# Nyström attention and a gated MLP: Newton inverses of batches 3+4 and 5+6 taken together, query weights kept unsplit until late, squares summed sooner

## The chip, the cores and the metric

One core of one Trainium2 chip. The metric is the device time of one execution in microseconds. "L563" and the like below are line numbers of the kernel file; PE is TensorE, DVE VectorE, ACT ScalarE, POOL GpSimd, SP SyncE (here it only issues DMAs).

## The reference

```python
# q, k, v: 8 batches x 8 heads x 576 tokens x 64; m = 32 landmarks of 18 tokens
q_lm, k_lm = means of q and k over the 18 tokens of each landmark
A, Bm, C = sm(q, k_lm), sm(q_lm, k_lm), sm(q_lm, k)          # softmax of scale*a@b.T
Z = Bm.T / (norm1(Bm) * norminf(Bm) + 1e-6)
for _ in range(6):
    Z = 2 * Z - Z @ Bm @ Z
x = (A @ Z @ C @ v)                                          # -> 4608 tokens x 512
xn = x / sqrt(mean(x * x) + 1e-6) * rms_g
out = (silu(xn @ w_gate) * (xn @ w_val)) @ w_out             # 512 -> 1536 -> 512
```

All of it is float32. The kernel gets this precision on PE by writing a number as a sum of two fp32r parts (hi and lo) and taking three products: hi by hi, hi by lo, lo by hi.

## The kernel before, in words

**Two parts.** The first part, which the change touches, runs the attention of all 8 batches and, mixed into it, the MLP of the first 4 of 12 blocks of 128 hidden units, for all tokens. The tokens come in 9 chunks of 512 (chunk i needs the attention of batches up to i, each of 576 tokens); eight chunks, 0 to 7, are run in this part by `mlp_chunk`. A chunk is 144 matmuls of 128x512: four blocks with 12 for the gate (psg) and 12 for the value (psv), then 48 for the output (pso). Its first matmul reads xhi, the hi part of the normalized tokens of kk = 0, its second xlo. The second part (the remaining blocks, from about 505 us on) is not touched.

**The attention of a batch** is a chain of steps; a batch's 8 heads form two groups g of 4 heads.

- `stage1(b, g)`: landmarks lmT (L342, sums on DVE of q and k, 128x1152 each), the next group's loads of q, k and v, then the scores sC and sA (16 small matmuls and 4 for psB), maxima mx (L376), E = exp(sC) on ACT, Bm (L392), and tA, sA transposed by DVE (L395).
- `back(b, g)`: softmax of tA: mA (L406), subtraction on POOL (L407), exp on ACT, sums, product on POOL (L414), transposition to AT (L416), and its split into AS, hi by ACT (L418) and lo by DVE (L419); transposes of E on PE (sE, sF), and pCV = C v, scaled into PV (L443).
- `newton(b)`: once both groups are through stage1, the start of Z, p0 on PE; once both groups are through back, five steps of 8 small matmuls (pn, 32x96) and one DVE operation (L498), which carry Z and Z C v together; a sixth for the product alone; then pW, split into Whi and Wlo.
- `second(b)`: pO (24 matmuls, AS by Whi and Wlo), copied by ACT into xr (L554), squared on ACT into sq; pss, the sum of squares over channels (8 matmuls); sqT, its transposition (L563); pms, which adds up four partial rows (L569); then on DVE ms, r, a reciprocal square root by ten small operations (L571 to L581), Rb, Rt (L583, L585), and xr scaled in place, four operations (L587). xr is stored to DRAM (xd, L591), and `finish` casts it to xhi on ACT (L614) and subtracts for xlo on DVE and POOL (L616).

**What sets the order.** Each engine runs its instructions in the order in which the program gives them. The steps above are generators, called streams; a `Mixer` keeps a clock, adds 0.216 for each MLP matmul (`MMT`), and after each lets one stream go on whose time has come. What a stream yields is how much work it added and how long it then waits; these waits are constants such as `OWL` (7.0: the wait between the last pO of a batch and its pss, times a slack of 1.3). Streams also wait for stages: stage1 of batch b for the Newton steps of batch b - 2, second(b) for newton(b) and for chunk b - 1 to have begun. After chunk i's last matmul the mixer is drained until second(i + 1) is through. The streams of second and newton run at high priority.

**Memory.** PE's results of the attention go through 5 banks of PSUM (tag pa), those of the MLP through 3 (tag pg). xr, E, tA, q/k and v have two buffers each, AT one, AS four.

Of the kernel before, what the change touches and what calls it, by code (L numbers as in the profile page):

```python
# [35 lines left out]
OWL = 7.0  # L36
# [13 lines left out]
TAB = 2  # L50
# [25 lines left out]
TINY = 1.0513759e-09  # L76


@with_exitstack
def nystrom_moe_kernel(  # L80
# [47 lines left out]
    VZ = cst.tile([P, G, 3 * D], F32, name="VZ")  # L128
# [169 lines left out]
    with tc.tile_pool(name="ap", bufs=1, side="right") as ap, tc.tile_pool(  # L298
# [36 lines left out]
        def stage1(b, g):  # L335
            nt = state[b]
            qk = loaded.pop((b, g))
            vt, vl_ = loaded.pop((b, g, "v"))
# [7 lines left out]
            if b > 0 and nxt[0] < B:  # L346
                load_qk(*nxt)
                load_v(*nxt)
# [31 lines left out]
            E = ap.tile([P, S], F32, name="E", tag="E", bufs=2)  # L380
# [4 lines left out]
            eb = sm.tile([P, M], F32, name="eb", tag="eb")  # L385
# [6 lines left out]
            (nc.scalar.mul if BMA else nc.vector.tensor_scalar_mul)(nt["Bm"][:, g, :], eb, rs[:, 1:2])  # L392
            tA = ap.tile([P, NB, M], F32, name="tA", tag="tA", bufs=TAB)
            for e in range(2):
                nc.vector.transpose(  # L395
                    tA[:, e * (NB // 2) : (e + 1) * (NB // 2), :].rearrange("p n m -> p (n m)"),
                    sA[e],
                )
            yield 1.3, 0.0
            if g == 1:  # L400
                stage["front"] = b

            def back():
                yield -BW * mix.slack
                mA = sm.tile([P, NB], F32, name="mA", tag="mA")
                nc.vector.tensor_reduce(mA, tA, axis=AX.X, op=ALU.max)  # L406
                nc.gpsimd.tensor_sub(tA, tA, mA.unsqueeze(2).broadcast_to([P, NB, M]))  # L407
                nc.scalar.activation(tA, tA, AF.Exp, scale=SC)
                sumA = sm.tile([P, NB], F32, name="sumA", tag="sumA")
                nc.vector.tensor_reduce(sumA, tA, axis=AX.X, op=ALU.add)  # L410
                nc.vector.tensor_scalar_add(sumA, sumA, 1e-9)
                rA = sm.tile([P, NB], F32, name="rA", tag="rA")
                nc.vector.reciprocal(rA, sumA)
                nc.gpsimd.tensor_mul(tA, tA, rA.unsqueeze(2).broadcast_to([P, NB, M]))  # L414
                AT = ap.tile([P, S], F32, name="AT", tag="AT", bufs=ATB)
                nc.vector.transpose(AT, tA.rearrange("p n m -> p (n m)"))  # L416
                AS = ap.tile([P, 2, S], F32R, name="AS", tag="AS", bufs=ASB)
                nc.scalar.copy(AS[:, 0], AT)  # L418
                nc.vector.tensor_sub(AS[:, 1], AT, AS[:, 0].bitcast(F32))  # L419
                nt["AT"][g] = AS  # L420

                sE = pa.tile([P, 4, P], F32, name="sE", tag="pa")
                for ch in range(4):
                    tp(sE[:, ch], E[:, ch * P : (ch + 1) * P], ident)
                sF = pa.tile([2 * M, P], F32, name="sF", tag="pa")
                tp(sF, E[:, 4 * P :], ident)
                ET = ap.tile([P, 4, P], F32, name="ET", tag="ET", bufs=ETB)
                EL = ap.tile([2 * M, P], F32, name="EL", tag="EL", bufs=ETB)
                nc.scalar.copy(ET, sE)
                nc.scalar.copy(EL, sF)  # L430
                yield 0.65, SW2
                pCV = pa.tile([P, D], F32, name="pCV", tag="pa")
                for ch in range(5):
                    for h in range(4):
                        r = slice(h * M, (h + 1) * M)
                        mm(
                            pCV[r, :],
                            ET[:, ch, r] if ch < 4 else EL[:, r],
                            vt[:, h, ch, :] if ch < 4 else vl_[:, h, :],
                            start=(ch == 0),  # L440
                            stop=(ch == 4),
                        )
                (nc.scalar.mul if CVA else nc.vector.tensor_scalar_mul)(nt["PV"][:, g, M:], pCV, rs[:, 0:1])  # L443
                yield 0.85, 0.2
                done[b] = done.get(b, 0) + 1
                if done[b] == 2:
                    stage["first"] = b

            mix.add(back())
# [9 lines left out]
        def newton(b):  # L459
            nt = state[b]  # L460
            Bm = nt["Bm"]
            BT = sm.tile([P, 2, M], F32, name="BT", tag="BT", bufs=1)
# [28 lines left out]
            yield 0.35, 0.0
            while stage["first"] < b:
                yield -0.3
            yield 0.0, NS
            for _ in range(5):
                pn = bmm(PV[:, :, :M], PV, M + D, "pn")
                PVn = sm.tile([P, 2, M + D], F32, name="PV", tag="PV", bufs=3)
                nc.vector.scalar_tensor_tensor(PVn, PV, 2.0, pn, op0=ALU.mult, op1=ALU.subtract)  # L498
# [3 lines left out]
            nc.vector.scalar_tensor_tensor(  # L502
                VZ[:, :, D : 2 * D], PV[:, :, M:], 2.0, pn, op0=ALU.mult, op1=ALU.subtract
            )
            yield 0.45, NP
            Whi = sm.tile([P, 2, P], F32R, name="Whi", tag="Whi", bufs=1)
            Wlo = sm.tile([P, 2, P], F32R, name="Wlo", tag="Wlo", bufs=1)
            pW = pa.tile([P, 2, P], F32, name="pW", tag="pa")
            for g in range(2):
# [12 lines left out]
            nt["W"] = Whi, Wlo  # L522
            yield 0.5, WW

        def new_state(b):
            state[b] = {
                "Bm": sm.tile([P, 2, M], F32, name="Bm", tag="Bm"),
                "PV": sm.tile([P, 2, M + D], F32, name="PV", tag="PV", bufs=3),
                "AT": [None, None],
            }  # L530

        def first(b):
            new_state(b)
            for g in range(2):
                yield from stage1(b, g)
# [3 lines left out]
        def second(b):  # L539
            nt = state.pop(b)  # L540
            (Whi, Wlo), ATs = nt["W"], nt["AT"]
            xr = ap.tile([P, NK, S], F32, name="xr", tag="xr", bufs=2)
            sq = ap.tile([P, NK, S], F32, name="sq", tag="sq", bufs=1)
            for g in range(2):
                po = [[pa.tile([P, HS], F32, name="pO", tag="pa") for j in range(2)] for e in range(2)]
                for e in range(2):
                    for n, (w, a) in enumerate(((Whi, 0), (Whi, 1), (Wlo, 0))):
                        for j in range(2):
                            r = slice(j * D, (j + 1) * D)
                            cols = slice(e * HS, (e + 1) * HS)  # L550
                            mm(po[e][j], w[r, g], ATs[g][r, a, cols], start=(n == 0), stop=(n == 2))
# [125 lines left out]
        mix.add(newtons(), True)  # L677
        mix.add(early.stream(WAIT0, NCV))
# [375 lines left out]
```

## Time and profile before

| what | value |
|---|---|
| time, median of 3 runs | 1066.85 us (1066.61 to 1067.96) |
| profiled execution | 1064.71 us, span 1062.8 us |
| chunks 0 to 3 begin at | 67.10, 134.10, 200.60, 268.80 us |
| chunk 7, without attention | 443.60 to 476.20 us |
| mean granted clock of PE | 0.961 |

A row of the timeline is start, duration, engine, line, operation, result and sources, shapes, count, and in brackets the idle time of the engine ahead of it and what ended that. A row of the windows has for each engine its busy time, then the granted clock of PE (1.00 is full), the share of DMA and GB/s. The waits list what PE waited for: total, number, the longest. A matmul's printed duration overlaps with the next, so the distance between two starts is its cost.

### The profile page before, as it was taken

How to read it: one execution, taken by the hardware profiler on the slowest of the kernel's cores; microseconds unless marked ns; L12 is line 12 of the kernel's file. 1: busy time of each engine (PE TensorE's matmuls, PEld its weight loads, DVE VectorE, ACT ScalarE, POOL GpSimd, SP SyncE). 2: the span in 40 equal slices, each digit the busy share in tenths (PEclk: the TensorE clock that was granted, in tenths of full speed). 3: DMA queues.
4: the chain of work that ended last, by engine and by line, in shares of the span. 5: the costliest groups of instructions: out<-in, count | busy, mean ns of one | idle time of the engine just before them, and what ended most of it. 6: DMA issues, size and time to landing. Idle time of an engine off the chain costs nothing.

```text
span 1062.8 us, 17582 instructions
## 1 busy us (share of the span) xinstructions
PE 992.8 (93%) x6918; PEld 833.9 (78%) x6918; DVE 743.4 (70%) x1503; ACT 486.7 (46%) x990; POOL 89.5 (8%) x86
## 2 busy tenths in 40 slices
PE   5639689989989999999999999999999999999998
PEld 3326466556767777787989899998999989899997
DVE  7799586797494551988995675747897475675743
ACT  3534556555454543455645352433744334352431
POOL 2243121211020210100000000000000000000000
PEclk7659889999999999999999999999999999999999
DMA  9244343434140211543533505134250432505122
GB/s 335 100 150 136 133 164 105 153 104 163 43 142 11 86 45 40 187 145 119 189 123 135 178 1 179 51 129 155 64 178 21 159 96 83 179 1 178 50 70 80
DMA packets 62946, 123.82 MB, mean 117 GB/s; under 512 B 5520, under 2 KB 27024, under 8 KB 61840
## 3 DMA queue, kind: packets, MB, share of 16 engines
q1 hardware_dynamic: 62864, 122.71, 34.0%
q8 instruction: 54, 0.88, 0.3%
q14 instruction: 28, 0.23, 0.1%
HBM read 84.94 MB, written 37.75 MB: 115 GB/s over the span
## 4 chain that ended last, share of the span: by engine, by line
PE 72%; DVE 15%; DMA 6%; issue 2%; ACT 2%; POOL 2%; SPq 0%; ACTq 0%; POOLq 0%; DVEq 0%
PE pso L141 23%; PE px L141 18%; PE pz L141 9%; PE psg L141 6%; PE psv L141 5%; PE pw L141 5%; DMA qk<-in_q_dram 2%; PE pO L141 2%; DMA srawv<-in_moe_w_val_dram 1%; DVE lmT L342 1%; PE pn L141 1%; DVE xr L587 1%; DVE h L275 1%; PE sC L141 1%; PE pss L141 1%
## 5 line engine op out<-in xcount | busy, mean ns | idle before, releaser
L141 PE MATMUL pso<-whio,h 128*128 128x512 f32 x288 | 96.2, 402 | 5.8 <-DVE h L275 4.7
L141 PE MATMUL pso<-solo,h 128*128 128x512 f32 x432 | 100.4, 390 | 0.0
L829 ACT CAST x<-xf 128x768 fp32r<-128x768 f32 x84 | 68.1, 833 | 69.7 <-DVE xf L847 54.2
L141 PEld LDWEIGHTS pso<-solo,h 128*128 128x128 f32 x432 | 81.0, 188 | 16.3
L141 PE MATMUL pso<-sowhio,h 128*128 128x512 f32 x288 | 90.9, 390 | 0.0
L141 PE MATMUL psg<-xhi,whig 128*128 128x512 f32 x144 | 60.7, 421 | 25.6 <-ACT xhi L614 25.6
L945 DVE TENSOR_TENSOR ob<-ob,pso 128x512 f32<-128x512 f32 x72 | 48.8, 684 | 49.1 <-PE pso L141 48.1
L830 DVE TENSOR_TENSOR x<-xf,x 128x768 fp32r<-128x768 f32 x84 | 79.2, 953 | 5.0 <-ACT x L829 5.0
L877 DVE TENSOR_TENSOR h<-c,h 128x384 fp32r<-128x384 f32 x96 | 53.2, 555 | 37.3 <-ACT h L876 37.2
L898 ACT COPY c<-px 128x384 f32<-128x384 f32 x48 | 23.1, 481 | 108.6 <-PE px L141 108.6
L141 PEld LDWEIGHTS pso<-whio,h 128*128 128x128 f32 x288 | 53.4, 188 | 20.4 <-DVE h L275 6.0
L876 ACT CAST h<-c 128x384 fp32r<-128x384 f32 x96 | 49.4, 515 | 34.5 <-DVE c L887 28.3
L141 PE MATMUL psg<-xlo,whig 128*128 128x512 f32 x144 | 60.6, 421 | 4.7 <-DVE xlo L616 4.0
L141 PEld LDWEIGHTS pso<-sowhio,h 128*128 128x128 f32 x288 | 54.1, 188 | 11.0
L141 PE MATMUL psg<-xhi,wlog 128*128 128x512 f32 x144 | 60.5, 420 | 0.0
L141 PE MATMUL psv<-xhi,wlov 128*128 128x512 f32 x144 | 58.1, 403 | 0.0
L141 PE MATMUL px<-x,swfs0c 128*128 128x384 f32 x288 | 58.0, 335 | 0.0
L141 PE MATMUL psv<-xlo,whiv 128*128 128x512 f32 x144 | 58.0, 403 | 0.0
L141 PE MATMUL px<-x,swfs1c 128*128 128x384 f32 x288 | 57.8, 334 | 0.1
L141 PE MATMUL px<-x,swfs2c 128*128 128x384 f32 x288 | 57.8, 335 | 0.0
L141 PE MATMUL psv<-xhi,whiv 128*128 128x512 f32 x144 | 57.8, 401 | 0.0
L141 PE MATMUL pso<-wloo,h 128*128 128x512 f32 x144 | 57.4, 398 | 0.0
(224 smaller groups left out, 2231.6 us busy)
## 6 DMA issues: line engine op xcount, KB each, us to landing
xd<-xr SPq DMA_DIRECT2D x8, 1152.0 KB, 4.3
pd<-ob SPq DMA_DIRECT2D x36, 256.0 KB, 2.1
xf<-xd SPq DMA_DIRECT2D x8, 1152.0 KB, 7.5
ob<-pd SPq DMA_DIRECT2D x36, 256.0 KB, 3.5
pe<-ob SPq DMA_DIRECT2D x36, 256.0 KB, 2.6
ob<-pe SPq DMA_DIRECT2D x36, 256.0 KB, 2.8
out_dram<-ob SPq DMA_DIRECT2D x36, 256.0 KB, 2.7
vt<-in_v_dram SPq DMA_DIRECT2D x16, 512.0 KB, 4.0
```

The source lines that it names most:

```text
L141: tc.keep_in_program_order(nc.tensor.matmul(*args, **kw))
L275: nc.vector.tensor_sub(h2, s, h1.bitcast(F32))
L342: nc.vector.tensor_reduce(lmT[:, z], qk[z].rearrange("p h (m c) -> p h m c", c=LM), axis=AX.X, op=ALU.add)
L587: last = nc.vector.scalar_tensor_tensor(xr[:, kk], xr[:, kk], gsb[:, kk : kk + 1], Rt, op0=ALU.mult, op1=ALU.mult)
L829: nc.scalar.copy(t[:, 0], src)
L830: nc.vector.tensor_sub(t[:, 1], src, t[:, 0].bitcast(F32))
L876: nc.scalar.copy(hi, s)
L877: nc.vector.tensor_sub(lo, s, hi.bitcast(F32))
L898: nc.scalar.copy(c1, px)
L945: nc.vector.tensor_add(ob, ob, bank.pop(t))
```

## The change

- `GROUPS`: newton is run for batches 0, 1, 2, (3, 4), (5, 6), 7; for a pair the tiles hold four groups of heads, and each step has 16 matmuls and one DVE operation of twice the elements. stage1 runs for both batches of a pair before newton's steps end.
- For batches from 3 on, `back` runs once for both groups: the softmax of tA is one operation of 128x1152 instead of two of 128x576 on each engine, sE has 8 and pCV 40 matmuls in a row, and PV is scaled by one multiplication. Here the loads of v come behind pCV and not in stage1.
- AT stays unsplit in float32 with three buffers (both groups); a new stream `splits` makes AS from it, with one buffer, once the batch is through back and pO of the batch before is given out.
- `OWL` goes from 7.0 to 3.0. xr has one buffer, tA and E one (of both groups).
- The gates that let stage1 and the last product of newton go on are new.

```diff
-OWL = 7.0
+OWL = 3.0
-TAB = 2
+TAB = 1
+XRB = 1
+GROUPS = ((0,), (1,), (2,), (3, 4), (5, 6), (7,))
+BOTH = 3
+SW3 = 2.6
+BW2 = 5.5
...
-                load_v(*nxt)
+                if nxt[0] <= BOTH:
+                    load_v(*nxt)
...
+            if b < BOTH:
+                mix.add(back(b, nt, g, 1))
+            elif g == 1:
+                mix.add(back(b, nt, 0, 2))
...
-                (nc.scalar.mul if CVA else nc.vector.tensor_scalar_mul)(nt["PV"][:, g, M:], pCV, rs[:, 0:1])
+            nc.vector.tensor_mul(
+                nt["PV"][:, at + g0 : at + g0 + n, M:], pCV[:, gsl], nt["rs"][:, gsl, 0:1].broadcast_to([P, n, D])
+            )
+            if n == 2 and b + 1 < B:
+                for g in range(2):
+                    load_v(b + 1, g)
...
+        def splits():
+            for b in range(B):
+                while stage["first"] < b or stage["small"] < b - 1:
+                    yield -0.3
+                nt = state[b]
+                AS = nt["AS"] = ap.tile([P, 2, 2, S], F32R, name="AS", tag="AS", bufs=1)
+                for g in range(2):
+                    nc.scalar.copy(AS[:, 0, g], nt["AT"][:, g])
+                    nc.vector.tensor_sub(AS[:, 1, g], nt["AT"][:, g], AS[:, 0, g].bitcast(F32))
+                stage["split"] = b
...
+            while stage["small"] < group[0] - 1:
+                yield -0.3
...
-            xr = ap.tile([P, NK, S], F32, name="xr", tag="xr", bufs=2)
+            xr = ap.tile([P, NK, S], F32, name="xr", tag="xr", bufs=XRB)
...
+                while i > 0 and stage["newton"] < GROUPS[i - (group[0] > 2)][-1]:
+                    yield -0.3
+                new_state(group[0])
+                for b in group:
+                    while b > 2 and (stage["second"] < max(1, b - 3) or (b == 4 and stage["newton"] < 2)):
+                        yield -0.3
+                    yield from stage1(b, 0)
+                    yield from stage1(b, 1)
...
-                while stage["newton"] < b or stage["chunk"] < b - 1:
+                while min(stage["newton"], stage["split"]) < b or stage["chunk"] < b - 1:
```

How the rows move is seen on PE and DVE. On PE before, in the output matmuls (pso) of chunk 1, stand batch 2's sums of squares (pss, pms) and Newton steps of batch 3 (pn):

```order
L141 MATMUL pss<-sq,ones 32x288 x8
L141 MATMUL pso<-whio_1054,h_1816 128x512
L141 MATMUL pn<-PV 32x96 x8
L141 MATMUL pso<-wloo_1055,h_1816 128x512
L144 MATMUL sE<-ident,E 128x128 x4
L144 MATMUL sF<-ident,E 64x128
L141 MATMUL pso<-whio_1054,h_1816 128x512
L141 MATMUL pn<-PV 32x96 x8
L141 MATMUL pso<-whio_1098,h_1952 128x512
L141 MATMUL pms<-sqT,sel 128x18
L141 MATMUL pso<-wloo_1099,h_1952 128x512
```

After pms come 17 more MLP matmuls of chunk 1. In the new order the same place, up to chunk 2's first matmul (psg), reads:

```order
L146 MATMUL pss<-sq,ones 32x288 x8
L146 MATMUL pso<-whio_1044,h_1674 128x512
L146 MATMUL pso<-whio_1088,h_1801 128x512
L146 MATMUL pso<-wloo_1089,h_1801 128x512
L146 MATMUL pso<-whio_1088,h_1801 128x512
L146 MATMUL pso<-whio_1139,h_1918 128x512
L146 MATMUL pso<-wloo_1140,h_1918 128x512
L146 MATMUL pso<-whio_1139,h_1918 128x512 x2
L146 MATMUL pso<-wloo_1140,h_1918 128x512
L146 MATMUL pso<-whio_1139,h_1918 128x512
L146 MATMUL pms<-sqT,sel 128x18
L146 MATMUL psg<-xhi_1402,whig_428 128x512
```

The sums have moved to the chunk's end: pms is the last row ahead of the next chunk. On PE before, batch 3's sums stand in the middle of chunk 2, among the gate and value matmuls of its blocks:

```order
L141 MATMUL pss<-sq,ones 32x288 x8
L141 MATMUL psv<-xhi_1467,wlov_468 128x512
L141 MATMUL pCV<-vt_2044,ET 32x64 x16
L141 MATMUL pCV<-vl_2045,EL 32x64 x4
L141 MATMUL psv<-xhi_1467,whiv_467 128x512
L141 MATMUL psv<-xlo_1468,whiv_467 128x512
L141 MATMUL psv<-xhi_1467,wlov_468 128x512
L141 MATMUL psg<-xhi_1467,whig_826 128x512
L141 MATMUL psg<-xlo_1468,whig_826 128x512
L141 MATMUL pms<-sqT,sel 128x18
L141 MATMUL psg<-xhi_1467,wlog_827 128x512
```

In the new order they stand at the end of chunk 2, with chunk 3's first matmul and batch 4's pO behind them:

```order
L146 MATMUL pss<-sq,ones 32x288 x8
L146 MATMUL pso<-whio_1088,h_2585 128x512
L146 MATMUL pso<-wloo_1089,h_2585 128x512
L146 MATMUL pso<-whio_1088,h_2585 128x512
L146 MATMUL pso<-whio_1139,h_2792 128x512
L146 MATMUL pso<-wloo_1140,h_2792 128x512
L146 MATMUL pso<-whio_1139,h_2792 128x512 x2
L146 MATMUL pso<-wloo_1140,h_2792 128x512
L146 MATMUL pso<-whio_1139,h_2792 128x512
L146 MATMUL pms<-sqT,sel 128x18
L146 MATMUL psg<-xhi_2189,whig_428 128x512
L146 MATMUL pO<-AS,Whi 128x288 x4
```

Batch 3's pms, too, is now the last row of its chunk. On DVE before, around batch 2's ms, the rows are the end of Newton steps (PV, L498), softmax and splitting of batch 4 (AT, AS):

```order
L563 STREAM_TRANSPOSE sqT<-pss 128x288
L413 RECIPROCAL rA<-sumA 128x18
L563 STREAM_TRANSPOSE sqT<-pss 128x288
L498 SCALAR_TENSOR_TENSOR PV<-PV,pn 128x192
L416 STREAM_TRANSPOSE AT<-tA 128x576
L498 SCALAR_TENSOR_TENSOR PV<-PV,pn 128x192
L571 TENSOR_SCALAR ms<-pms 128x18
L419 TENSOR_TENSOR AS<-AT,AS 128x576
```

In the new order, between batch 2's sqT and ms stand the landmark sums (lmT) of batch 5's first group and three small rows of batch 4's softmax:

```order
L601 STREAM_TRANSPOSE sqT<-pss 128x288 x2
L347 TENSOR_REDUCE lmT<-qk_2138 128x64
L400 TENSOR_TENSOR ss<-ss 128x1
L401 TENSOR_SCALAR ss<-ss 128x2
L402 RECIPROCAL rs<-ss 128x2
L347 TENSOR_REDUCE lmT<-qk_2138 128x64
L609 TENSOR_SCALAR ms<-pms 128x18
L403 TENSOR_SCALAR Bm<-eb,rs 128x32
```

Both lmT now come ahead of ms.

More of the change, by code (lines that the diff above doesn't have):

```diff
@@ L127, in nystrom_moe_kernel @@
     nc.vector.memset(ones, 1.0)
[L128 removed]
+    VZ = cst.tile([P, 2 * G, 3 * D], F32, name="VZ")
     nc.gpsimd.memset(VZ, 0.0)
@@ new lines, in back @@
+        def back(b, nt, g0, n):
+            gs = range(g0, g0 + n)
+            gsl = slice(g0, g0 + n)
+            yield -(BW if n == 1 else BW2) * mix.slack
+            ta = nt["tA"][:, gsl]
+            tA = ta.rearrange("p g n m -> p (g n) m")
+            mA = sm.tile([P, 2 * NB], F32, name="mA", tag="mA")[:, : n * NB]
+            nc.vector.tensor_reduce(mA, tA, axis=AX.X, op=ALU.max)
+            nc.gpsimd.tensor_sub(tA, tA, mA.unsqueeze(2).broadcast_to([P, n * NB, M]))
+            nc.scalar.activation(tA, tA, AF.Exp, scale=SC)
+            sumA = sm.tile([P, 2 * NB], F32, name="sumA", tag="sumA")[:, : n * NB]
+            nc.vector.tensor_reduce(sumA, tA, axis=AX.X, op=ALU.add)
+            nc.vector.tensor_scalar_add(sumA, sumA, 1e-9)
+            rA = sm.tile([P, 2 * NB], F32, name="rA", tag="rA")[:, : n * NB]
+            nc.vector.reciprocal(rA, sumA)
+            nc.gpsimd.tensor_mul(tA, tA, rA.unsqueeze(2).broadcast_to([P, n * NB, M]))
+            nc.vector.transpose(nt["AT"][:, gsl].rearrange("p g s -> p (g s)"), tA.rearrange("p n m -> p (n m)"))
+            ET = ap.tile([P, 2, 4, P], F32, name="ET", tag="ET", bufs=ETB)
+            EL = ap.tile([2 * M, 2, P], F32, name="EL", tag="EL", bufs=ETB)
+            for g in gs:
@@ L431, in back @@
-                yield 0.65, SW2
-                pCV = pa.tile([P, D], F32, name="pCV", tag="pa")
+                    tp(sE[:, ch], nt["E"][:, g, ch * P : (ch + 1) * P], ident)
+                nc.scalar.copy(ET[:, g], sE)
+            sF = pa.tile([2 * M, 2, P], F32, name="sF", tag="pa")
+            for g in gs:
+                tp(sF[:, g], nt["E"][:, g, 4 * P :], ident)
+            nc.scalar.copy(EL[:, gsl], sF[:, gsl])
+            yield 0.65 * n, SW2 if n == 1 else SW3
+            pCV = pa.tile([P, 2, D], F32, name="pCV", tag="pa")
@@ L433, in back @@
+            for g in gs:
+                vt, vl_ = loaded.pop((b, g, "v"))
                 for ch in range(5):
@@ L442, in back @@
                         )
[L443 to L449, printed above, removed]
+            at = nt["at"]
+            nc.vector.tensor_mul(
[4 more added lines that the diff above has]
+                    load_v(b + 1, g)
+            yield 0.85 * n, 0.2
+            done[b] = done.get(b, 0) + n
+            if done[b] == 2:
+                stage["first"] = b
+        def splits():
[8 more added lines that the diff above has]
+                stage["split"] = b
         def bmm(lt, rhs, n, nm):
-            ps = pa.tile([P, 2, n], F32, name=nm, tag="pa")
-            for g in range(2):
+            w = lt.shape[1]
+            ps = pa.tile([P, w, n], F32, name=nm, tag="pa")
+            for g in range(w):
                 for h in range(4):
@@ L457, in bmm, with newton @@
             return ps
[L459 to L462, printed above, removed]
+        def newton(group):
+            nt = state[group[0]]
+            n = 2 * len(group)
+            Bm = nt["Bm"][:, :n]
+            BT = sm.tile([P, 4, M], F32, name="BT", tag="BT", bufs=1)[:, :n]
             nc.vector.transpose(
@@ L521, in newton @@
             nc.vector.tensor_sub(Wlo, pW, Whi.bitcast(F32))
-            nt["W"] = Whi, Wlo
+            for b in group:
+                state[b]["W"] = Whi, Wlo
             yield 0.5, WW
         def new_state(b):
[L526 to L535, printed above, removed]
+            group = next(gr for gr in GROUPS if b in gr)
+            if b == group[0]:
+                tiles = {
+                    "Bm": sm.tile([P, 4, M], F32, name="Bm", tag="Bm", bufs=2),
+                    "PV": sm.tile([P, 4, M + D], F32, name="PV", tag="PV", bufs=3),
+                }
+                for i, c in enumerate(group):
+                    state[c] = dict(tiles, at=2 * i)
         state = {}
```

115 lines of the change are left out of this document (46 added, 69 removed).

## The prediction

> **What bounds the kernel now.** I read the profile's page first (span, busy shares), then the stretches of the eight chunk starts, then TensorE's waits, then the timelines around the largest of them.
>
> ```profile
> span 1062.8 us, 17582 instructions
> PE 992.8 (93%) x6918; PEld 833.9 (78%) x6918; DVE 743.4 (70%) x1503; ACT 486.7 (46%) x990; POOL 89.5 (8%) x86
> ```
>
> TensorE (PE) is the bound, but not evenly. The change touches only the first part, up to the end of chunk 7; the next table has chunks 0, 1, 2, 3 and, last, chunk 7, which holds no attention.
>
> ```profile
> core 0: us, PE busy (x) PEld busy (x) DVE busy (x) ACT busy (x) POOL busy (x), PEclk, DMA share, GB/s
> 67.10:134.10 67.00, 52.05 (x480) 36.50 (x480) 51.52 (x111) 31.81 (x68) 20.48 (x15) 0.86 0.41 134
> 134.10:200.60 66.50, 62.87 (x788) 42.65 (x788) 53.15 (x133) 34.44 (x75) 11.83 (x11) 0.94 0.36 120
> 200.60:268.80 68.20, 60.97 (x695) 41.25 (x695) 57.55 (x148) 40.02 (x86) 17.13 (x16) 0.95 0.44 155
> 268.80:317.50 48.70, 46.00 (x433) 33.66 (x432) 31.97 (x84) 23.90 (x55) 7.92 (x9) 1.00 0.27 90
> 443.60:476.20 32.60, 32.60 (x145) 27.03 (x144) 29.56 (x64) 18.06 (x38) 0.00 (x0) 1.00 0.59 186
> ```
>
> A chunk is 144 MLP matmuls, so 32.6/144 = 0.226 us each when nothing intervenes. PE idles 14.95, 3.63, 7.23 and 2.70 us in chunks 0 to 3, 28.5 in all. The waits name where:
>
> ```profile
> PE psg L141 <- ACT xhi L614: 25.6, 3, 13.9
> PE pn L141 <- DVE PV L498: 8.8, 9, 1.6
> PE psg L141 <- DVE xlo L616: 4.0, 3, 1.8
> ```
>
> The largest kind is a chunk's first matmul waiting for the normalized tokens (xhi). It appears three times: before chunk 0 (13.9), before chunk 1 and, small, before chunk 2.
>
> ```profile
> 122.40 0.40 PE L141 MATMUL pms<-sqT,sel 128*128 128x18 f32 x2
> 134.06 0.79 PE L141 MATMUL psg<-xhi,whig 128*128 128x512 f32 x1 [11.26 <-ACT xhi L614]
> 137.73 0.80 PE L141 MATMUL psg<-xlo,whig 128*128 128x512 f32 x1 [1.82 <-DVE xlo L616]
> 200.59 0.50 PE L141 MATMUL psg<-xhi,whig 128*128 128x512 f32 x1 [0.44 <-ACT xhi L614]
> 201.90 0.50 PE L141 MATMUL psg<-xlo,whig 128*128 128x512 f32 x1 [0.81 <-DVE xlo L616]
> ```
>
> Between pms (sum of squares) and xhi lies a serial chain on VectorE and ScalarE. At chunk 1 nothing covers it. At chunk 2 the MLP matmuls that stand behind pms on PE cover all but 0.44 us. At chunk 3 pms stands in the middle of chunk 2, so nothing is waited for. **This is where the change acts**, as the order shows: afterwards pms of batches 1, 2 and 3 is the last PE instruction ahead of chunks 1, 2 and 3.
>
> **The change part by part.** The bare chain, from batch 4, where VectorE (DVE) had little else:
>
> ```profile
> 289.15 0.29 PE L141 MATMUL pms<-sqT,sel 128*128 128x18 f32 x2
> 289.48 0.18 DVE L571 TENSOR_SCALAR ms<-pms 128x18 f32<-128x18 f32 x1 [1.57 <-PE pms L141]
> 293.02 0.65 DVE L271 TENSOR_TENSOR s<-s,psv 128x512 f32<-128x512 f32 x1
> 293.59 3.48 DVE L587 SCALAR_TENSOR_TENSOR xr<-xr,gsb,Rt 128x576 f32<-128x576 f32 x4
> 132.63 0.77 DVE L587 SCALAR_TENSOR_TENSOR xr<-xr,gsb,Rt 128x576 f32<-128x576 f32 x1
> 133.44 0.77 ACT L614 CAST xhi<-xr 128x448 fp32r<-128x448 f32 x2 [1.79 <-DVE xr L587]
> ```
>
> From pms to the first xr is 4.44 us, with one foreign instruction of 0.57 (from 293.02 to 293.59) in it: 3.87 bare. From the first xr to the first psg are 134.06 - 132.63 = 1.43 more. A wholly exposed chain thus costs about 3.87 + 1.43 = 5.3, less the 0.1 of pms itself: 5.2 us of idle PE.
>
> Idle PE is also paid for a second time, by the granted clock:
>
> ```profile
> 124.80:141.90 17.10, 6.03 (x16) 4.53 (x17) 17.10 (x42) 7.69 (x19) 6.02 (x6) 0.50 0.34 135
> 199.90:203.30 3.40, 2.15 (x9) 0.97 (x8) 3.36 (x7) 3.38 (x10) 2.27 (x2) 1.00 0.90 345
> 203.30:206.70 3.40, 3.40 (x37) 2.17 (x45) 1.58 (x3) 2.44 (x6) 2.03 (x3) 0.50 0.77 314
> 240.80:244.30 3.50, 3.50 (x30) 2.12 (x32) 2.58 (x9) 1.53 (x2) 0.21 (x1) 0.51 0.80 261
> ```
>
> After a stretch with only 2.15 of 3.40 us busy, the next 3.40 ran at 0.50: 1.7 us lost. After chunk 1's long wait the clock stayed at 0.50 until 141.90, 7.8 us past the restart, of which 1.82 were idle anyway: 3.0 lost. For the new waits I take 2.0, between the two.
>
> The Trainium skill's page "TensorE: Matmul & The Clock Gate", section "What's actually happening", gives a drop to half clock only after at least one idle window of about 3.4 us. The trace differs: 1.25 us of idle in two pieces (0.44 and 0.81) were followed by half clock. By the page chunk 2 would have paid nothing for it before, and my sum would be 1.7 us higher.
>
> *Chunk 2, batch 2's chain.* On DVE both lmT reductions of batch 5 now stand between sqT and ms.
>
> ```profile
> 120.49 0.92 DVE L563 STREAM_TRANSPOSE sqT<-pss 128x288 f32<-128x288 f32 x2 [0.98 <-PE pss L141]
> 181.21 0.33 SPq L323 DMA_DIRECT2D qk<-in_q_dram  x1
> 186.19 1.35 DVE L342 TENSOR_REDUCE lmT<-qk 128x64 f32<-128x1152 f32 x1 [1.19 <-DMA qk<-in_q_dram]
> ```
>
> Behind pss PE has ten MLP matmuls, 2.3 us, and then pms. DVE has sqT 0.92, two lmT 2.7 and three tiny ones, about 0.3: ms starts 3.9 us after pss, 1.3 later than a bare chain would. If lmT must also wait for its load, it is worse: the load's buffer comes free with batch 4's first scores, nine MLP matmuls (2.0 us) and pss (0.6, estimated from half of the 16-matmul row quoted below) ahead. The load takes 186.19 - 181.21 = 4.98, so lmT starts 2.4 after pss, not 0.9: 1.5 more. Idle PE 5.2 + 1.3 = 6.5 to 8.0; I take 7.2. The wait for xlo follows it, 1.82 at chunk 1 and 0.81 at chunk 2 before; I take 1.8, since all four xr are again ahead of it. With 2.0 for the clock: 11.0. Before it was 0.44 + 0.81 + 1.7 = 2.95. **+8.0**, bounds +5 and +10.
>
> *Chunk 3, batch 3's chain.* Nothing stands in it on DVE: 5.2 idle, 0.4 for xlo (batch 4's pO, now between the first two MLP matmuls, covers most of it), 2.0 clock. Before: nothing. **+7.6**, bounds +6 and +10.
>
> *Chunk 1, batch 1's chain.* Batch 2's second scores move behind the chunk's start, and so does the DVE work that was woven into this chain:
>
> ```profile
> 122.62 0.45 DVE L376 TENSOR_REDUCE mx<-sC 128x1 f32<-128x288 f32 x1
> 123.06 0.48 DVE L395 STREAM_TRANSPOSE tA<-sA 128x288 f32<-128x288 f32 x1
> 127.74 0.73 DVE L406 TENSOR_REDUCE mA<-tA 128x18 f32<-128x576 f32 x1
> ```
>
> With mx and tA twice, for the two halves of the scores, these are 2.6; with some ten small ones of the same group (estimated at 0.15 each, from ms's 0.18) about 4.0 leave the chain. One AS subtraction, estimated at 0.7 from mA of the same width, enters behind the first xr. The scores and transposes that were free in the idle time, estimated at 1.8 of PE, now cost time inside chunk 1. 4.0 - 1.8 - 0.3: **-1.9**, bounds -3 and 0.
>
> *Inside the chunks.* The wait of 3.16 in chunk 2 goes, since batches 3 and 4 scale their PV in one operation each and no longer ahead of scores there:
>
> ```profile
> 239.88 0.43 PE L141 MATMUL sA<-qk,lmT 64*32 64x288 f32 x1 [3.16 <-DVE PV L443]
> ```
>
> With its half clock (240.80 to 244.30, 1.7) that is 4.9; next late are the scores' own banks, which I put at 1.4 of it (bounds 0 and 3): **-3.5**. Every piece of attention put between MLP matmuls costs two uneven steps:
>
> ```profile
> 333.80 0.39 PE L141 MATMUL psv<-xhi,whiv 128*128 128x512 f32 x1
> 334.12 1.18 PE L141 MATMUL pss<-sq,ones 128*32 128x288 f32 x16
> 335.23 0.50 PE L141 MATMUL psv<-xlo,whiv 128*128 128x512 f32 x1
> 335.57 0.40 PE L141 MATMUL psv<-xhi,wlov 128*128 128x512 f32 x1
> ```
>
> 0.32 and 0.34 in place of 0.226: 0.21 a piece. The order has about 104 pieces in chunks 0 to 6 before, 94 after: **-2.1**. Of the pn waits (8.8) half the batches lose half: a quarter, **-2.2**; wider PV operations (twice the elements) hold the rest.
>
> *At nothing.* The POOL operations double in width:
>
> ```profile
> L407 POOL TENSOR_TENSOR tA<-tA,mA 128x576 f32<-128x576 f32 x16 | 18.5, 1159 | 87.7 <-DVE mx L379 42.8 <-DVE mA L406 35.2 <-DVE rs L391 3.5
> ```
>
> Uncovered, each would cost 1.16 more, but dozens of MLP matmuls lie between them and the first use of AT. The v loads move behind pCV of the batch before, well ahead of their use; uncovered, that is one load of about the 4.98 above. Late splitting of AT moves its ScalarE casts and DVE subtractions without adding any; a pO that had to wait for them would lose one of each, estimated at 0.7 apiece as above. At the head of chunk 0 one mA more precedes the chain: **+0.4** (0 to 0.73).
>
> Sum: -1.9 + 8.0 + 7.6 - 3.5 - 2.1 - 2.2 + 0.4 = **+6.3 us**. The profiled execution took 1064.71 (span 1062.8 and 1.9 around it), so 1071.0 there; the median of the runs shown is 2.1 above it: **1073.1**. About 0.2% (2.1 us) is what a measurement can tell from no change.
>
> **The rivals.** *Faster: the idle inside the chunks goes.* Of the 28.5 us, 11.26, 1.82 and 0.81 belong to starts of chunks and 0.44 to chunk 2's, so about 14.2 lie inside chunks 0 to 3, and 1.7 with the second half-clock stretch: 15.9. I credit 3.5 + 2.2 = 5.7 of it. Merged and later steps could free more of DVE, busy 57.55 of 68.20 us in chunk 2. It decides from 12.0 (even) on; at 14.1 faster by 0.2%; all of it gives 1063. Against: most DVE work only moves, and chunk 3's idle is not touched by it. Chance 0.28.
>
> *No change: it cancels* at 12.0 of 15.9, or with both new exposures at their low bounds (+11 for two rather than 15.6) and a little more inside: about 1067. Chance 0.17.
>
> *Much slower: single buffers.* xr has one buffer now, so batch 4's pO, right behind chunk 3's first matmul, can't be evicted before batch 3's store has read xr:
>
> ```profile
> xd<-xr SPq DMA_DIRECT2D x8, 1152.0 KB, 4.3
> ```
>
> The store follows the last xr (2.9 us after the first, by 3.48 less the 0.57 foreign) and takes 4.3: evictions wait until 7.2 after the first xr, 5.8 after chunk 3 starts. The second half of pO stands 13 MLP matmuls on, about 3.0 us: PE waits some 2.8. With both chains at their upper bounds (+4.4) that is 1080. Within my slower chance of 0.55 I give it 0.15.
>
> **How the numbers follow.** Forecast 0.40, the much slower rival 0.15, no change 0.17, faster 0.28. The range reaches from 1061.5, past the faster rival's 1063, to 1080.5. The likeliest case's own range is 1069 to 1078.
>
> **What would show it.** Right: waits of psg for xhi of 6.5 to 8 at chunk 2's start and about 5 at chunk 3's, each with a stretch at half clock; 3.16 for PV gone. The forecast fails if those starts show under 3 us, or if chunks 1 to 3 have lost over 10 us inside.

## The result and the profile after

The changed kernel took 1086.16 us (median of 4 runs, 1084.3 to 1087.57), the kernel before 1067.4 in the same comparison: a ratio of 1.0175, 95% interval 1.0156 to 1.0193. It is slower by 18.8 us; the forecast was slower by 6.3, and the time lies above the range, which ended at 1080.5.

The page of the changed kernel, its span, busy times and clock by slices (to compare with the first rows of the prediction):

```profile
span 1084.2 us, 17468 instructions
PE 998.5 (92%) x6918; PEld 841.7 (78%) x6918; DVE 735.7 (68%) x1437; ACT 484.7 (45%) x978; POOL 89.5 (8%) x76
```

The span grew by 21.4 us, PE's busy time by 5.7: most of the loss is idle PE. Chunks 0 to 3, and chunk 7, by windows of the changed kernel:

```profile
core 0: us, PE busy (x) PEld busy (x) DVE busy (x) ACT busy (x) POOL busy (x), PEclk, DMA share, GB/s
68.32:129.33 61.01, 49.77 (x439) 35.24 (x439) 44.04 (x89) 27.68 (x58) 15.60 (x12) 0.89 0.35 119
129.33:202.23 72.90, 59.41 (x654) 41.26 (x654) 48.01 (x119) 37.15 (x78) 11.77 (x8) 0.90 0.38 129
202.23:277.90 75.67, 62.40 (x742) 44.33 (x742) 48.52 (x103) 34.38 (x69) 12.55 (x8) 0.86 0.32 109
277.90:345.50 67.60, 61.42 (x670) 44.24 (x671) 51.31 (x125) 31.75 (x75) 16.14 (x12) 0.87 0.26 96
463.80:497.50 33.70, 33.26 (x146) 26.83 (x145) 31.29 (x68) 17.47 (x38) 0.00 (x0) 1.00 0.49 152
```

Chunk 0 begins 1.2 us later than before. Chunks 0 to 3 take 277.2 us, 26.8 more than before; chunks 4 to 6 take 463.80 - 345.50 = 118.3 instead of 126.1, 7.8 less, since attention is through sooner; chunk 7 takes 1.1 more. That is the 21.4. The starts of the chunks, on PE:

```profile
129.33 0.79 PE L146 MATMUL psg<-xhi,whig 128*128 128x512 f32 x1 [9.51 <-ACT xhi L652]
132.13 0.80 PE L146 MATMUL psg<-xlo,whig 128*128 128x512 f32 x1 [2.00 <-DVE xlo L654]
202.23 0.80 PE L146 MATMUL psg<-xhi,whig 128*128 128x512 f32 x1 [6.35 <-ACT xhi L652]
205.51 0.79 PE L146 MATMUL psg<-xlo,whig 128*128 128x512 f32 x1 [2.48 <-DVE xlo L654]
277.90 0.80 PE L146 MATMUL psg<-xhi,whig 128*128 128x512 f32 x1 [5.04 <-ACT xhi L652]
281.15 0.80 PE L146 MATMUL psg<-xlo,whig 128*128 128x512 f32 x1 [0.71 <-DVE xlo L654]
```

These are the waits forecast, near the sizes forecast. On DVE, both lmT stand ahead of batch 2's ms as foreseen, the second after a short wait for its load:

```profile
195.90 1.35 DVE L347 TENSOR_REDUCE lmT<-qk 128x64 f32<-128x1152 f32 x1 [0.35 <-DMA qk<-in_k_dram]
```

What was not forecast are waits inside the chunks, and what the granted clock adds to them. First the five longest waits of chunks 1, 2 and 3 other than the starts, as PE's rows show them, then the stretches of half clock in which PE worked, from chunk 1's start on, as windows:

```profile
154.69 0.29 PE L146 MATMUL p<-BT 32*32 32x32 f32 x12 [2.77 <-DVE tA L405]
224.13 0.65 PE L146 MATMUL p<-BT 32*32 32x32 f32 x32 [1.77 <-ACT E L393]
242.79 0.86 PE L146 MATMUL pn<-PV 32*32 32x96 f32 x32 [1.94 <-DVE PV L533]
315.88 1.12 PE L149 MATMUL sE<-ident,E 128*128 128x128 f32 x4 [2.79 <-ACT ET L442]
336.09 1.50 PE L146 MATMUL pn<-PV 32*32 32x96 f32 x32 [1.77 <-DVE PV L533]
```

```profile
127.96:131.38 3.42, 0.79 (x1) 0.29 (x1) 3.42 (x5) 2.03 (x6) 0.62 (x1) 0.50 0.00 0
131.38:134.79 3.41, 2.38 (x5) 1.48 (x6) 1.63 (x5) 2.24 (x5) 3.41 (x3) 0.50 0.73 303
134.79:138.20 3.41, 3.41 (x10) 2.67 (x9) 0.00 (x0) 0.32 (x1) 1.15 (x2) 0.51 0.11 43
155.27:158.68 3.41, 3.41 (x9) 2.65 (x8) 3.41 (x7) 1.09 (x5) 0.00 (x0) 0.51 0.03 7
199.64:203.06 3.42, 0.80 (x1) 0.29 (x1) 3.35 (x6) 1.39 (x4) 0.07 (x1) 0.50 0.00 0
203.06:206.47 3.41, 0.96 (x2) 0.83 (x3) 3.41 (x4) 2.66 (x6) 3.24 (x4) 0.50 0.31 130
206.47:209.88 3.41, 3.41 (x37) 1.72 (x39) 1.41 (x4) 0.22 (x1) 0.72 (x1) 0.51 0.53 216
223.54:226.95 3.41, 2.82 (x37) 2.34 (x38) 3.31 (x6) 1.53 (x7) 0.90 (x1) 0.50 0.00 1
226.95:230.36 3.41, 3.41 (x9) 2.64 (x8) 3.41 (x10) 0.00 (x0) 0.00 (x0) 0.51 0.01 2
244.02:247.43 3.41, 3.41 (x38) 2.30 (x37) 3.40 (x7) 0.04 (x1) 0.00 (x0) 0.51 0.02 5
274.74:278.15 3.41, 0.25 (x1) 0.25 (x1) 3.24 (x8) 0.76 (x3) 0.00 (x0) 0.50 0.08 28
278.15:281.56 3.41, 2.70 (x14) 1.92 (x15) 3.41 (x4) 2.23 (x7) 2.91 (x3) 0.50 0.21 86
281.56:284.98 3.42, 3.42 (x9) 2.68 (x9) 1.80 (x3) 0.00 (x0) 1.19 (x2) 0.51 0.63 259
315.69:319.11 3.42, 2.53 (x32) 1.59 (x36) 3.38 (x13) 1.49 (x6) 0.17 (x1) 0.50 0.01 2
319.11:322.52 3.41, 3.41 (x32) 2.67 (x23) 2.35 (x6) 2.90 (x10) 3.03 (x3) 0.51 0.00 0
336.17:339.59 3.42, 3.42 (x37) 2.56 (x37) 1.85 (x8) 0.00 (x0) 2.13 (x1) 0.51 0.00 0
```

Every one of the five waits is followed by one or two windows at half clock. I count half of the busy time in such a window as lost (an estimate: it takes all of PE's work as going at the granted clock): (0.79 + 2.38 + 3.41)/2 = 3.3 us at chunk 1's start, (0.80 + 0.96 + 3.41)/2 = 2.6 at chunk 2's, (0.25 + 2.70 + 3.42)/2 = 3.2 at chunk 3's, and half of the other seven, 11.2, behind the five waits inside, where the kernel before lost 1.7.

The first of the five shows how one buffer of tA makes such a wait. POOL, then DVE, before PE's wait ends:

```profile
152.15 1.16 POOL L433 TENSOR_TENSOR tA<-tA,rA 128x576 f32<-128x576 f32 x1 [7.88 <-DVE mx L390]
153.34 0.78 DVE L434 STREAM_TRANSPOSE AT<-tA 128x576 f32<-128x576 f32 x1 [1.05 <-POOL tA L433]
154.16 0.48 DVE L405 STREAM_TRANSPOSE tA<-sA 128x288 f32<-128x288 f32 x1
```

tA has one buffer now. The next batch's sA can be transposed into it only when the old tA is through POOL's product and DVE's AT. So DVE stands 1.05 us behind POOL, the bank of PSUM with sA comes free some 1.9 us late (this wait and AT's 0.78), and p, which needs a bank, holds up PE and the MLP matmuls behind it.

### The profile page after: what moved, and what is told of

It is laid out like the page before. It is cut to its first block, busy times and chain, and to the rows that moved or that the text cites. A ratio compares the mean times of both kernels' runs of the same rounds, so it can differ in the third digit from the quotient of the medians.

```text
span 1084.2 us, 17468 instructions
## 1 busy us (share of the span) xinstructions
PE 998.5 (92%) x6918; PEld 841.7 (78%) x6918; DVE 735.7 (68%) x1437; ACT 484.7 (45%) x978; POOL 89.5 (8%) x76
## 4 chain that ended last, share of the span: by engine, by line
PE 60%; DVE 7%; DMA 3%; ACT 1%; issue 1%; POOL 0%; ACTq 0%; SPq 0%; DVEq 0%; POOLq 0%
PE pso L146 22%; PE px L146 17%; PE pz L146 8%; PE pw L146 4%; PE psv L146 3%; PE psg L146 3%; DMA srawo<-in_moe_w_out_dram 1%; DVE sw L773 1%; DMA pd<-ob 1%; DVE sw L776 1%; DMA srawv<-in_moe_w_val_dram 1%; DVE x L871 1%; PE pn L146 1%; PE pO L146 1%; DVE sw L769 0%
## 5 line engine op out<-in xcount | busy, mean ns | idle before, releaser
L146 PE MATMUL psg<-xlo,whig 128*128 128x512 f32 x144 | 63.0, 437 | 7.2 <-DVE xlo L654 6.5
L146 PEld LDWEIGHTS psg<-xhi,whig 128*128 128x128 f32 x144 | 29.8, 207 | 42.8 <-ACT xhi L652 35.6
```

The costliest lines, as they stand in the source:

```text
L146: tc.keep_in_program_order(nc.tensor.matmul(*args, **kw))
```

## The experiments

Theory A: waits inside the chunks, from single buffers and doubled steps that hold PSUM banks, each with a price in clock besides. Theory B: the uncovered starts of chunks 2 and 3 alone. Theory C: pairing as such (doubled steps, crowded stage1) is slow. Ratios are to the kernel before in the same comparison; us are ratio by 1068.

**Two buffers for tA.**

```diff
-TAB = 1
+TAB = 2
...
-                nt["AT"] = ap.tile([P, 2, S], F32, name="AT", tag="AT", bufs=3)
+                nt["AT"] = ap.tile([P, 2, S], F32, name="AT", tag="AT", bufs=2)
```

> The changed kernel with two buffers for tA (as one batch had before) and two instead of three for AT; PE's order of steps is the same. Theory A (the extra time inside the chunks comes from single buffers and doubled steps that hold PSUM banks, and each such wait costs the clock besides): the wait of p for tA's transposition in chunk 1 (2.77 us) goes and the half-clock window behind it (155.58 to 159, 1.7 us): 3 to 5 us faster than the changed kernel, about 1082. Theory B (the loss lies in the exposed starts of chunks 2 and 3 alone): within 1 us of the changed kernel, 1086.

Measured: 1.0080 (1.0058 to 1.0102), 10 us faster than the changed kernel, more than expected. The wait of p for tA is gone, and so is that for E in chunk 2:

```profile
150.79 0.33 PE L146 MATMUL p<-BT 32*32 32x32 f32 x16
```

Chunk 1 takes 2.9 us less and chunk 2 5.3. With pairs, one buffer of tA less is worth half of the loss (AT gave one up in this run). B alone is out.

**Idle PE kept busy at the starts.**

```diff
+WARM = {1: 42, 2: 28, 3: 22}
...
             mix.drain(lambda: stage["second"] > i)
+            if i + 1 in WARM:
+                ps = pg.tile([P, T], F32, name="psw", tag="pg")
+                for _ in range(WARM[i + 1]):
+                    mm(ps[:, :P], ident, ident, start=True, stop=True)
```

> The changed kernel with idle matmuls of 128x128 (ident by ident, 42, 28 and 22 of them, result unused) behind pms and ahead of the first matmul of chunks 1, 2 and 3: the waits stay, but PE is busy in them. Theory A with the clock as a price of its own: the half-clock stretches behind those three starts (8.6 us lost by the windows: 3.0, 2.3 and 3.3) mostly go, 5 to 8 us faster than the changed kernel, about 1079. Rival: the clock follows something else (power, DMA, the kind of matmul), or the waits for xlo just behind throw it back anyway: within 1.5 us of the changed kernel.

Measured: 1.0114 (1.0081 to 1.0147), 6.5 us faster. The three half-clock windows at chunk 3's start are gone, and two of the three at chunk 1's and at chunk 2's. Not all of the gain need be clock: the waits for xlo add up to 8.2 us in place of 6.5, but pn's 1.94 in chunk 2 shrank to 0.29, and its half-clock window went with it. At chunk 3's start xlo is still waited for 1.76 us, and yet this window and the next ran at full clock:

```profile
274.59:278.00 3.41, 1.79 (x16) 1.12 (x14) 3.41 (x4) 2.82 (x8) 2.31 (x3) 1.00 0.00 0
```

**The same in the kernel before** (chunks 0 and 1: 52 and 48).

> The kernel before with idle matmuls (result unused) ahead of chunks 0 and 1: 52 and 48, in waits of 13.9 and 11.3 us. Theory A with the clock as its own price: of 4 and 3 us lost there at half clock some 4 to 5 come back, about 1063. Rival: the same within 1.5 us, 1067.

Measured: 0.9996 (0.9980 to 1.0012): nothing. The windows behind chunk 0's start, in the kernel before and then in this one:

```profile
66.82:70.24 3.42, 1.76 (x3) 1.12 (x4) 3.42 (x8) 3.03 (x9) 2.35 (x1) 0.50 0.25 105
70.24:73.65 3.41, 2.72 (x7) 1.65 (x6) 3.41 (x5) 0.00 (x0) 3.41 (x3) 0.50 0.58 241
```

```profile
66.67:70.09 3.42, 1.46 (x3) 0.85 (x4) 3.42 (x7) 3.33 (x9) 2.04 (x1) 0.58 0.18 76
70.09:73.50 3.41, 2.72 (x7) 1.71 (x6) 3.41 (x7) 0.00 (x0) 3.41 (x3) 0.50 0.66 270
```

The filled idle ran at full clock, but the short waits that the idle matmuls didn't cover (up to 2.2 us for xhi, 2.6 for xlo) took the clock down in the same windows. So my expectation was wrong where it counted all idle: here the short waits cost as much clock as the long one. Both results fit a price that goes by windows; with no gain here, the 6.5 us there are the only sign of it in the time.

**Unpaired**, all else as changed.

```diff
-GROUPS = ((0,), (1,), (2,), (3, 4), (5, 6), (7,))
+GROUPS = tuple((i,) for i in range(8))
```

> The changed kernel with every batch's inverse iteration by itself (all of GROUPS single); the merged softmax, the late split, single buffers and OWL stay. Batch 3's sums come in the middle of chunk 2 then, so chunk 3's start is covered; four MLP matmuls stand behind pms of batch 2. Theory B (starts): chunk 3's 5.0 + 0.7 idle and 3.3 clock go, 0.9 of chunk 2's: about 10 us faster than the changed kernel, 1076. Theory A: the same 10 less 2 to 3 us for 16 more pieces between MLP matmuls, while the waits for banks in chunks 1 and 2 stay: 1078 to 1079. Theory C (the doubled steps of the pairs are themselves what is slow): 15 us or more faster.

Measured: 0.9981 (0.9965 to 0.9997), 21 us faster than the changed kernel, twice what B had and more than twice A's. C stood, for the moment.

**OWL alone**, in the kernel before (7.0 to 3.0).

> The kernel before with OWL 3.0 alone. Sums are squared sooner, which lets later batches' steps come sooner too; batch 2's pms falls to the 133rd matmul of chunk 1 with ten MLP matmuls behind it (2.4 us) instead of 17 (before: 0.44 + 0.81 us of idle at chunk 2). Theory A and B alike: the start of chunk 2 loses about 2 us more, other starts are covered, and 123 pieces instead of 104 cost up to 4 us: 1068 to 1073. Rival (OWL is what made the changed kernel slow): 1078 or more.

Measured: 1.0056 (1.0034 to 1.0077), 6 us slower. Chunk 2 then waits 5.61 us for xhi, not 0.44: the sooner sums of batch 1 let batch 2's scores slip behind chunk 1's start, and batch 2's sums nearer to chunk 1's end.

**Unpaired, with two buffers for tA**, then with OWL back at 7.0, and filled.

> The changed kernel unpaired and with two buffers for tA (two for AT): both earlier edits together. Theory A: the wait of p for tA in chunk 1 (2.8 us) and the half-clock window after it (1.7) go as they did with pairs: 4 to 5 us faster than unpaired alone, about 1062. Rival (the buffer's gain came from waits that only pairs have): within 1 us of unpaired alone, 1066.5.

> Unpaired, two buffers for tA (1063.7), with OWL back at 7.0, which alone cost 6 us in the kernel before when lowered to 3.0. If sooner sums are bad as such: 5 us faster, 1058. If OWL only shifts which steps collide, as I hold: within 3 us, with the stage1 steps of batch 2 free in chunk 1's start again but batch 2's sums at the end of chunk 1 (8 matmuls behind pms instead of 4).

> As the last, with idle matmuls (result unused) ahead of the first matmul of chunks 0, 1 and 2: 52, 42 and 20. The waits of 14.3, 9.5 and about 4.5 us stay. Theory A with the clock as its own price: most of the half-clock stretches behind these starts goes (about 4, 3 and 2 us lost), less what the xlo waits throw back: 4 to 7 us faster than the last kernel, about 1057. Rival (the earlier gain by filling came from elsewhere): within 1.5 us of the last kernel.

Measured: 0.9957 (0.9941 to 0.9974), faster than the kernel before. It is 2.6 us faster than unpaired alone: without pairs, tA's second buffer is worth a quarter of the 10 us that it gave with them. With OWL 7.0 it is 1.0054 (1.0036 to 1.0072), 10 us slower where I had expected at most 3, while alone OWL 7.0 was the better: chunk 2's start waits 8.80 us for xhi then, not 3.90. What OWL is worth depends on what stands around it; it decides which start is uncovered. Filling gave nothing (0.9969, 0.9949 to 0.9988), where 4 to 7 us were expected.

**Softmax steps by group of heads again** (`BOTH = 8`), with pairs.

> The changed kernel with pairs, but the softmax steps by group of heads as before (BOTH = 8): POOL 128x576 instead of 128x1152, sE 4 at a time. Theory A (doubled steps hold the banks): the waits of sE for ET in chunk 3 (2.8 + 0.7) and their half-clock windows (3 us) go; ten MLP matmuls stand behind pms of batches 2 and 3, which covers 2.3 us of both exposed starts: 8 to 11 us faster than the changed kernel, about 1076; ten more pieces cost 2 of it. Theory B (starts alone): 4 to 5 faster, 1081. Theory C (pairs of stage1 crowded into chunk 3 are what is slow): the wait in chunk 3 stays in another place, 1081 to 1084.

Measured: 1.0077 (1.0051 to 1.0103), 10.5 us faster than the changed kernel, as A had it; but half of A's reason is missing, since PE waits for a bank behind tA (2.6 and 4.2 us in all) stay. Chunk 2 takes 12.6 us less and chunk 3 7.5 more, so this run doesn't separate the theories.

**One pair at a time**, two buffers for tA.

> Two buffers for tA as before, and of the pairs only 5+6. Beside it stand both pairs (1077.5) and none (1063.7), 13.8 us apart. Theory A (the pair 3+4 costs by uncovering chunk 3's start, 9 us with the clock; what is left is crowding in chunk 3 by four stage1 steps): here chunk 3's start is covered as without pairs, two of the four stage1 steps fall in chunk 2: 1064 to 1067. Theory C (a pair is slow by itself, about 7 us each): 1070 to 1071.

> The same with only the pair 3+4. Batch 3's pms stands four MLP matmuls ahead of chunk 3, so 4 us of its chain are uncovered there, with xlo and two half-clock windows behind. Theory A: 8 to 12 us slower than without pairs, 1072 to 1076. Theory C: 1070 to 1071.

Measured: 5+6 alone 0.9972 (0.9957 to 0.9988), not to be told from none; 3+4 alone 1.0115 (1.0087 to 1.0143), 17 us slower than none, more than the 8 to 12 of theory A. C falls as a rule for every pair: 5+6 costs nothing. Chunk 3 without pairs, then with 3+4:

```profile
266.10:323.70 57.60, 55.56 (x664) 38.98 (x663) 45.52 (x111) 32.71 (x68) 12.19 (x8) 1.00 0.23 81
```

```profile
270.40:341.10 70.70, 63.66 (x702) 43.64 (x703) 54.56 (x130) 36.76 (x81) 15.98 (x12) 0.88 0.25 92
```

13.1 us longer: 5.0 more of idle, and 8.1 more of busy PE, most of it at half clock (1.00 against 0.88); chunk 2 takes 5.2 more, with 1.9 more of wait for xlo and, at its end, a wait of 3.70 for chunk 3's xhi that isn't there without the pair. With the pair, batch 3's sums wait for batch 4's softmax and end up at chunk 3's start.

**MLP matmuls held back.** This was the run to tell uncovered starts from pairs: the last 20 matmuls of chunks 0 to 2 go behind the next batch's sums, and pairs and buffers stay.

```diff
-            mix.fill(mlp_chunk(i, early, fs, *chunks.pop(i)))
+            rest = mlp_chunk(i, early, fs, *chunks.pop(i))
+            mix.fill(itertools.islice(rest, 144 - HELD.get(i, 0)))   # {0: 20, 1: 20, 2: 20}
             mix.drain(lambda: stage["second"] > i)
+            mix.fill(rest)
```

> The changed kernel, pairs and single buffers and all, with the last 20 MLP matmuls of chunks 0, 1 and 2 held back until the next batch's sums and norm are given out: pms of batches 1, 2 and 3 then has 20 matmuls (4.5 us) behind it. Theory B and A alike (the exposed starts, idle and clock): of 9.5, 6.4 and 5.0 us of idle 4.5 each may go, and at chunk 3 the half-clock stretches too: 10 to 16 us faster than the changed kernel, 1070 to 1076; a little is lost because pss now waits for the squares with nothing between. Theory C (pairing costs by what it does inside the chunks: crowding, banks): 4 to 8 faster, 1078 to 1082.

> The kernel with only the pair 3+4 (1081.0; without the pair 1063.7) with the same 20 matmuls held back in chunks 0 to 2. Theory A: the starts of chunks 2 and 3 are what the pair costs, 10 us of the 17 as idle and the rest as clock behind them and behind a wait of sE (2.5): 1067 to 1071. Theory C: 1075 or more.

Measured: 0.9995 (0.9980 to 1.0010), 19 us faster than the changed kernel; with only the pair 3+4 and two buffers 0.9895 (0.9860 to 0.9930), 23.5 us faster than the same without holding back. Both are more than expected. The starts of chunks 2 and 3 in the first of them, sums and first matmul:

```profile
181.42 0.29 PE L147 MATMUL pms<-sqT,sel 128*128 128x18 f32 x2
189.00 0.50 PE L147 MATMUL psg<-xhi,whig 128*128 128x512 f32 x1 [1.00 <-ACT xhi L653]
246.86 0.29 PE L147 MATMUL pms<-sqT,sel 128*128 128x18 f32 x2
252.20 0.50 PE L147 MATMUL psg<-xhi,whig 128*128 128x512 f32 x1 [0.40 <-ACT xhi L653]
```

6.35 and 5.04 us of wait became 1.00 and 0.40, and chunk 1's 9.51 became 4.00, a start that was uncovered before the change too. The 19 us are not the starts alone: chunks 0 to 2 take 25.5 us less, chunk 3 9.3 more. So uncovered starts are a large part of the loss. They are not all that the pair 3+4 costs: held back, it stands at 0.9895, and the unpaired kernel below, held back in chunks 0 and 1 (and with xhi first, which alone gave no clear gain), at 0.9803. So some 9 of its 17 us seem to be left, and no run says where they come from; a part of C may be right here.

**The remaining starts.** Unpaired, two buffers: the products with xhi first in a chunk's first gate block; with filling; with 20 held back in chunks 0 and 1; with 36 in chunk 0. Then 20 held back in chunk 0 of the kernel before.

```diff
+                terms = [(kk, j) for kk in range(NK) for j in range(3)]
+                if fi == 0 and nm == "g":
+                    terms.sort(key=lambda t: t[1] == 1)
...
```

> Unpaired, two buffers for tA, and in a chunk's first gate block the eight products with xhi ahead of the four with xlo, so that eight matmuls lie over the wait for xlo. Theory A: the xlo waits at chunks 0 to 2 (3.9 us in all) and POOL's 0.6 go, and with them a half-clock window at each start that they alone caused: 3 to 6 us faster than the same without it (1063.7), about 1059. Rival: the matmuls wait for the later parts of xhi instead, or the start is bound by DVE's chain: within 1.5 us.

> The last with idle matmuls ahead of chunks 0, 1 and 2 (52, 42 and 20, result unused). Filling alone gave nothing before, where the xlo waits stood right behind. Theory A (any window with a wait over about 1.2 us takes the clock from the next, however long the idle before it): with both kinds of wait covered the clock stays at 1.00 through the starts, 3 to 5 us faster than the last, about 1055. Rival (what slows the starts isn't the clock): within 1.5 us of the last.

> Unpaired, two buffers for tA, xhi products first (1062.7), with 20 matmuls held back in chunks 0 and 1, the two whose following start is still exposed (9.5 and 3.9 us). If the starts are idle that can be covered: 5 to 8 us faster, about 1056, the fastest so far. Rival (other chains come late in their place): within 2 us.

> The fastest so far (unpaired, two buffers for tA, xhi products first, 20 matmuls held back: 1047.0), with 36 instead of 20 in chunk 0, where 4.3 us of wait for xhi were left at chunk 1. If what is left can be covered: 3 to 4 us faster, about 1043. Rival (pss and pms then wait on the squares with nothing between, and the chain comes no sooner): within 2 us.

> The kernel before with the last 20 MLP matmuls of chunk 0 held back until batch 1's norm is given out; nothing else. Its one exposed start (chunk 1: 11.3 us idle, 1.8 for xlo, 3 at half clock) should lose some 5 to 8 us: 1060 to 1063. Rival (its chain is bound by DVE work woven in, which moves along): within 2 us, 1068.

Measured: 0.9948 (0.9928 to 0.9967) and 0.9930 (0.9907 to 0.9953), neither to be told from 0.9957; then 0.9803 (0.9773 to 0.9833), 1047.0 us, the fastest of all kernels here and faster than expected; 36 give the same (0.9802, 0.9787 to 0.9817). In the kernel before, holding back gave nothing (1.0012, 0.9997 to 1.0028), the rival's outcome:

```profile
121.80 0.58 PE L142 MATMUL pms<-sqT,sel 128*128 128x18 f32 x2 [1.21 <-DVE mx L380]
136.80 0.79 PE L142 MATMUL psg<-xhi,whig 128*128 128x512 f32 x1 [7.38 <-ACT xhi L615]
```

Its chain takes 15.0 us from pms to psg, 3.3 more than without holding back (122.40 to 134.06): on DVE, softmax rows, an AT, an AS, a Newton start and two lmT of 1.34 us are woven into it. Cover doesn't help where the chain itself is late.

## Why the prediction failed

**Right: the starts.** Chunk 2's: 7.2 + 1.8 + 2.0 = 11.0 expected, 6.35 + 2.48 + 2.6 = 11.4 in the trace. Chunk 3's: 5.2 + 0.4 + 2.0 = 7.6 expected, 5.04 + 0.71 + 3.2 = 9.0. Chunk 1's gave 1.3 back (9.51 + 2.00 + 3.3 against 11.26 + 1.82 + 3.0), 1.9 expected, though that sum takes off 0.3 without a source, beside an AS subtraction put at 0.7; the head of chunk 0 cost 1.2, not 0.4. Together +17.3 for +14.1 expected. Holding back bears it out: with the starts of chunks 1 to 3 covered the kernel is 19 us faster, if not by the starts alone.

**Wrong: the step "inside the chunks".** I credited 3.5 + 2.1 + 2.2 = 7.8 us of gain there. What is left of 21.4 after the starts is +4.1. The wait of 3.16 did go, as expected. But five new waits stood in for the old one: PE's idle inside chunks 0 to 3, starts apart, rose from 14.2 to 18.1 us, and by the windows 9.5 us more were lost to half clock (11.2 against 1.7). The rest came out some 9 us shorter, with the shorter chunks 4 to 6 in it; it isn't broken down further. Three faults made this step wrong by 12 us.

- An edit that I never priced: tA's buffers from two to one. The text followed xr's single buffer, which turned out harmless (PE's wait of pO for xr is 0.2 us in all, not 2.8), and passed over tA's, worth 10 us by the run with two (2.6 without pairs). Sum and bounds for what is inside had gains, and no way for it to lose.
- The clock was charged to the starts only. I had the price from the trace of before (1.7 us after 1.25 us of idle), and yet didn't ask what a new wait of 2 us would cost: in the five here its own length and, by the windows, 1.7 to 3.1 more.
- The term for pn (-2.2) took a quarter of 8.8 us. Only 3.2 of these lie inside the chunks, as the row below shows for 67.1 to 317.5 us; the other 5.6 come ahead of chunk 0, where nothing is paired. After the change pn waits 5.1 us inside (1.35, 1.94 and 1.77): +1.9 in place of -2.2.

```profile
PE pn L141 <- DVE PV L498: 3.2, 4, 0.9
```

**The rivals.** The faster one failed: idle inside chunks 1 to 3 grew. The much slower one named the right outcome with the wrong buffer. That batch 3's sums move to the end of chunk 2 because they wait for the pair was in the order and in the sum; that this one pair costs 17 us and the other nothing I learned only from the runs with one pair.

**Open.** The price of the clock is read from windows and may be too high: by them the changed kernel loses some 13 us more than the one before (23 against 10 from chunk 0's start on), but PE's busy time grew by 5.7 in all. Of four runs that filled idle PE one was clearly faster, with pairs. Unpaired with two buffers, filling took what the windows lose from 9.0 us to 5.4, but pn's waits grew from 4.1 to 7.4 and the time stayed. The three waits of sE and pn that remain in the run with two tA buffers were not taken away one by one, and why some 9 us of the pair 3+4 stay when matmuls are held back is not known.

## What to carry to other kernels

When work is merged, look first at which later step now waits for the last member, and whether that step has other work behind it on the bound engine: the serial chain of 5 us left a wait of 0.40 for xhi (and 1.59 for xlo) behind 20 matmuls, and cost 9 us with clock and all at the end of a stage. Price each buffer that goes, by the wait of the next writer and of all that queue behind that writer. If a stage ends in a chain of other engines, hold back some of the bound engine's own work for it; here that was worth 1.4 to 2.2% in three kernels, and nothing in a fourth whose chain itself came later.

## What the runs showed of the hardware

The half-clock windows of the changed kernel all lie on one grid of 3.41 us (155.27, 203.06, 206.47, 223.54 and so on). The Trainium skill's page "TensorE: Matmul & The Clock Gate", section "What's actually happening", has the window length and that it runs free. A window need not be idle for the next to be slow: behind a wait of 1.77 us (1.65 of 3.41 us busy) the clock fell. At half clock, 2.82 of 3.41 us busy (223.54 to 226.95) was followed by another slow window, while 3.04 of 3.40 in the trace of before, at full clock (206.70 to 210.10), was not.

```profile
206.70:210.10 3.40, 3.04 (x47) 2.00 (x31) 2.48 (x8) 2.51 (x5) 0.66 (x1) 1.00 0.46 150
302.35:305.76 3.41, 1.60 (x7) 0.86 (x5) 2.74 (x6) 2.47 (x8) 1.75 (x3) 1.00 0.65 266
305.76:309.18 3.42, 2.72 (x47) 1.84 (x48) 3.42 (x14) 0.69 (x2) 0.79 (x2) 1.00 0.20 77
```

But the busy time of a window alone doesn't decide. The last two rows are from the kernel before too: in them PE waits 2.50 us, 1.60 of 3.41 us are busy, and the next window is at full clock all the same. With its starts filled, the same place of that kernel (302.19 to 305.60, 1.55 busy) was followed by a window at 0.58. What tells the two apart, these runs don't show.
